# Block attention and cosine router on one core: paired first gathers, earlier key and embedding transposes, and logits in four column parts

## The chip, the cores and the metric

The kernel runs on one core of a Trainium2 chip. A core has a matrix engine (TensorE, "PE" in the profile, with its weight loads as "PEld"), VectorE (DVE), ScalarE (ACT), GpSimd (POOL) and SyncE (SP), which here does little but issue DMAs. Each engine runs its own instructions in order; semaphores tie them together. The metric is the device time of one execution in microseconds, the median of several runs. A profile is one execution more, with every instruction recorded.

## The reference, cut to what matters

```python
q, k, v: (4, 8, 768, 64)            # batch, heads, sequence, head size
mask: own block of 32 and its neighbours, first and last block rows and columns,
      and 3 sampled blocks per row of blocks
attn = softmax(where(mask, q @ k.T / 8, -1e9)) @ v
x = attn as (3072, 512)             # 8 heads side by side

xn = x / (norm(x) + 1e-6);  en = expert_emb / (norm(expert_emb) + 1e-6)
logits = xn @ en.T / tau            # (3072, 8)
expert_idx = argmax(logits);  gate = softmax(logits)[expert_idx]
out = gate * (relu(x @ w1[expert_idx]) @ w2[expert_idx])   # 8 experts, 512 -> 1024 -> 512
```

## The kernel before, in words

There are two large stages. The attention stage makes x and the routing; the expert stage gathers 128 rows of one expert at a time and sends them through that expert's two matrices. Everything is float32; one matrix product of that type is two pairs of a weight load and a matmul in the trace.

**Chunks, pairs and steps.** The 3072 rows are 24 chunks of 128 rows. Two chunks at the same place of two neighbouring sequences form a pair (`DUO = 2`), and a pair shares its block numbers. The order of chunks is `TURNS = [0, 2, 1, 3, 4, ...]`: the first chunks of the first two pairs come before their second chunks. `attention_fast` runs a loop of 25 steps `s`, in an order written out by hand: no scheduler moves anything, each engine gets its instructions in the order of the code. In step `s` four chunks are in work: `now` (scored in this step), `last` (its probabilities weigh the values), `past` (its rows x are transposed and its logits made) and `after` (its queries are transposed and its keys gathered, for the next step).

**Scores.** `score_near` makes the scores of the own and neighbouring blocks and of the two end blocks (tile `ac`, then `exp` into `pac`). `score_far` makes those of the sampled blocks (`dps`, then `pd`) from gathered keys `kg`, which `gather_k` copies together on GpSimd and VectorE out of the transposed keys `kt`. `turn_k(g)` transposes the keys of head pair `g` of a sequence (groups 0 to 3 are sequence 0, 4 to 7 sequence 1) into a bank of the two-bank ring `big`, which the scores use too; VectorE copies the even groups out, ScalarE the odd ones. `turn_q` transposes a chunk's queries.

**Weighing.** `weigh_far`, `weigh_near` and, for chunks at a sequence's end, `weigh_ends` multiply values by probabilities into `av` (all at L629). The far values come from HBM: `gather_v` issues one DMA for each sampled slot and block into a ring of two tiles, `vg`, one tile for each pair. Called with a third argument, it fetches for one chunk of the pair only (64 KB a DMA), without it for both (128 KB). The rows are runs of 256 bytes. All of these DMAs, and those for q, k, v, x and the weights, are issued by SyncE in the order of the code (`fetch_all`, L475 to L479), and a gather into `vg` waits until the products that read the tile two pairs before are done. A gather also needs its block number in a register first.

**Start of the stage.** Before the loop SyncE issues: keys of groups 0 to 3, values of two blocks, keys 4 and 5, the gathers of pair 0's first chunk, more values, keys 6 and 7, the gathers of pair 1's first chunk with the queries of the two second chunks between them, then the values of the second sequence, broken by the gathers of pair 0's second chunk, and at the end those of pair 1's second chunk. Keys 4 to 7 are transposed at the end of step 1, one after another, and only then are the keys for the next step gathered.

**Logits.** `normalize` divides by the sum of the probabilities into x and squares it on ScalarE into a tile `sq` for the norm. One step later `turn_x` transposes x into `xt`, and `chunk_logits` multiplies: the 128x128 parts of `xt` are the stationary operand, 8 columns of normalised embeddings `en` move, four products summed in one PSUM bank; ScalarE copies the (128, 8) result to `lg`. All small products of this stage share that one bank (`bank`, a ring of one tile). `build_experts` makes `en` in parts, called once before the loop, once in step 0 and twice in step 1. Its last two parts each transpose two pieces of the embeddings in that bank and copy them out.

**Routing** (`route`, `rank`, `dispatch_early`) is cut into pieces that hang on later steps; `planned(0)` runs such pieces in the middle of a step, `planned(1)` at its end.

Of the kernel before, what the change touches and what calls it, by code (L numbers as in the profile page):

```python
# [97 lines left out]
def build_consts(k):  # L98
    nc, pool = k.nc, k.const
    k.ones = pool.tile([P, P], F32, name="ones")  # L100
    nc.vector.memset(k.ones, 1.0)

    groups = k.ident.rearrange("p (g t) -> p g t", g=NG)
    k.mine = pool.tile([P, NG], F32, name="mine")
    nc.vector.reduce_sum(out=k.mine, in_=groups, axis=AX.X)
    no = iota(k, "group_no", [P, NG], [[1, NG]])
    k.group = pool.tile([P, 1], F32, name="group")
    nc.vector.tensor_tensor(out=no, in0=no, in1=k.mine, op=ALU.mult)
    nc.vector.reduce_sum(out=k.group, in_=no, axis=AX.X)
    k.ones_b = pool.tile([P, P], BF16, name="ones_b")  # L110
    nc.vector.memset(k.ones_b, 1.0)
    k.before = pool.tile([P, P], BF16, name="before")
    nc.gpsimd.memset(k.before, 1.0)
    nc.gpsimd.affine_select(out=k.before, in_=k.before, pattern=[[1, P]], compare_op=ALU.is_ge,
                            fill=0.0, base=-1, channel_multiplier=-1)
    k.rev = iota(k, "rev", [P, E], [[-1, E]], base=E)
    k.lane = iota(k, "lane", [P, P], [[1, P]])
    k.by_g = iota(k, "by_g", [P, NL + 1], [[G, NL + 1]])
    k.tile_no = iota(k, "tile_no", [P, NL], [[1, NL]])
    build_tokens(k, True)  # L120

    k.oh = pool.tile([P, NT, E], BF16, name="oh")
    k.rank = pool.tile([P, NT], F32, name="rank")
    k.seen = pool.tile([P, NT + 1, E], BF16, name="seen")
    nc.vector.memset(k.seen[:, 0, :], 0.0)
# [89 lines left out]
def build_experts(k):  # L215

    nc, pool = k.nc, k.setup
    emb, tau = k.emb_rows, k.tau_rows
    sq = pool.tile([E, DM], F32, name="emb_sq")
    nrm = pool.tile([E, 1], F32, name="emb_nrm")  # L220
    nc.scalar.activation(sq, emb, ACT.Square, accum_out=nrm)
    nc.gpsimd.tensor_tensor(out=nrm, in0=nrm, in1=k.half[0:E, 0:1], op=ALU.pow)
    yield
    nc.vector.tensor_scalar(out=nrm, in0=nrm, scalar1=1e-6, scalar2=tau[:, 0:1], op0=ALU.add, op1=ALU.mult)
    nc.vector.reciprocal(out=nrm, in_=nrm)
    nc.vector.tensor_scalar(out=emb, in0=emb, scalar1=nrm[:, 0:1], scalar2=None, op0=ALU.mult)
    yield
    k.en = k.const.tile([P, ND, E], F32, name="en")
    for some in (range(2), range(2, ND)):
        tp = bank(k, "tp")  # L230
        for c in some:
            nc.tensor.transpose(tp[:, c * E:(c + 1) * E], emb[:, c * P:(c + 1) * P], k.ident[0:E, 0:E])
        cols = slice(some.start * E, some.stop * E)
        nc.vector.tensor_copy(out=k.en.rearrange("p c e -> p (c e)")[:, cols], in_=tp[:, cols])
        yield


def load_pair(k, g, parts=(0, 1, 2)):
# [399 lines left out]
def weigh_near(k, n, turn):  # L638

    _, c, i = place(n)  # L640
    if turn == 0:
        k.av[n] = two_banks(k, "av"), set()
    e, st = k.pac[n], k.st_ring[n // DUO % 2]
    for hh in range(2 * turn, 2 * turn + 2):
        for h in (hh, hh + NPAIR):
            for half in (1,) if c == 0 else (0, 1):
                to = side(c, h, half)
                weigh(k, n, slice(D * to, D * (to + 1)), h, e[:, h // 2, half, D * (h % 2):D * (h % 2 + 1)],
                      st[:, half, i, h], turn == 1)
    if turn == 1:  # L650
        k.pac.pop(n)


def weigh_far(k, n, part):
# [14 lines left out]
def normalize(k, n):  # L669

    nc = k.nc
    b, c, i = place(n)
    s = n // DUO
    if i == 0:
        k.x[s] = k.xp.tile([P, DUO, ND, XE], F32, name="x", tag="x")
        k.nsq[s] = k.xp.tile([P, DUO], F32, name="nsq", tag="nsq")
        k.lg[s] = k.xp.tile([P, DUO, E], F32, name="lg", tag="lg")
    av = k.av.pop(n)[0].rearrange("p g (h w) -> p (g h) w", w=P)
    den = k.dens[:, n, :]
    nc.vector.tensor_scalar(out=den, in0=av[:, :, D], scalar1=1e-9, scalar2=None, op0=ALU.add)  # L680
    inv = k.xt_pool.tile([P, H], F32, name="inv", tag="inv")
    nc.vector.reciprocal(out=inv, in_=den)
    x = k.x[s][:, i, :, 0:P].rearrange("p j (h d) -> p j h d", h=2)
    half = NPAIR // 2
    if c:
        todo = [(slice(0, P), slice(0, P), slice(0, NPAIR))]
    else:
        todo = [(slice(0, P), slice(0, P), slice(0, half)), (slice(0, D), slice(D, P), slice(half, NPAIR)),
                (slice(D, P), slice(0, D), slice(half, NPAIR))]
    for to, at, pairs in todo:  # L690
        heads = slice(2 * pairs.start, 2 * pairs.stop)
        count = pairs.stop - pairs.start
        nc.vector.tensor_tensor(  # L693
            out=x[to, pairs], in0=av[at, heads, 0:D].rearrange("p (j h) d -> p j h d", h=2),
            in1=inv[at, heads].rearrange("p (j h) -> p j h", h=2).unsqueeze(3).broadcast_to(
                [at.stop - at.start, count, 2, D]), op=ALU.mult)
    sq = k.xt_pool.tile([P, ND, P], F32, name="sq", tag="sq", bufs=1)
    nc.scalar.activation(sq, k.x[s][:, i, :, 0:P], ACT.Square, accum_out=k.nsq[s][:, i:i + 1])


def turn_x(k, n):
# [6 lines left out]
    k.nc.vector.tensor_copy(out=t, in_=ps)  # L708


def chunk_logits(k, n):

    s, i = divmod(n, DUO)
    xt = k.xt.pop(n)
    ps = bank(k, "last_lg")
    for j in range(ND):
        k.nc.tensor.matmul(ps[:, 0:E], lhsT=xt[:, j], rhs=k.en[:, j, :], start=(j == 0), stop=(j == ND - 1))  # L717
    k.nc.scalar.copy(out=k.lg[s][:, i], in_=ps[:, 0:E])


# [25 lines left out]
def logits(k, x):  # L746
    nc, p = k.nc, k.rp
    lg = two_banks(k, "lg")[:, 0, 0:NC * E].rearrange("p (c e) -> p c e", e=E)
    for c2 in range(0, NC, 2):
        ps = k.big.tile([P, 2 * ND, P], F32, name="xt_ps", tag="big")  # L750
        for i in range(2 * ND):
            c, d = c2 + i // ND, i % ND
            nc.tensor.transpose(ps[:, i, :], x[:, c, d, 0:P], k.ident)
        xt = p.tile([P, 2 * ND, P], F32, name="xt")
        nc.vector.tensor_copy(out=xt, in_=ps)
        for c in (c2, c2 + 1):
            for d in range(ND):
                nc.tensor.matmul(lg[:, c, :], lhsT=xt[:, (c - c2) * ND + d, :], rhs=k.en[:, d, :],
                                 start=(d == 0), stop=(d == ND - 1))
    return lg  # L760

# [482 lines left out]
def attention_fast(n, ctx):  # L1244
# [40 lines left out]
    for vg in n.vg_ring:  # L1285
        nc.gpsimd.memset(vg[:, :, :, :, D:D + 1], 1.0)
    build_choice(n)
    fetch_all(n, gather_v(n, 0, 0), [])
    for m in range(2, NC):
        fetch_all(n, (), load_v(n, 0, m, 0))  # L1290
    turn_q(n, 0)
    for g in range(NPAIR):
        turn_k(n, g)
        if g + 6 < 2 * NPAIR:
            fetch_all(n, (), load_k(n, g + 6))
    fetch_all(n, gather_v(n, 1, 0), load_q(n, 0, 1) + load_q(n, 1, 1))
    for m in range(2):
        fetch_all(n, (), load_v(n, 0, m, 1))
    fetch_all(n, gather_v(n, 0, 1), [])
    for m in range(2, NC):  # L1300
        fetch_all(n, (), load_v(n, 0, m, 1))
    fetch_all(n, gather_v(n, 1, 1), [])
    build_bias(n)
    gather_k(n, 0)
    n.half = n.const.tile([P, NC], F32, name="half")
# [7 lines left out]
    nc.gpsimd.memset(zero, 0.0)  # L1313
    nc.sync.dma_start(n.x_dram[N:N + 1, :], zero)

    turning = {10: (8, 9), 11: (10, 11, 12), 12: (13, 14, 15)}
    keys_at = {2: (8, 9), 3: (10,), 4: (11,), 5: (12,), 6: (13,), 10: (14, 15)}
    values_at = {7: (0,), 8: (1,), 9: (2,), 11: (3,), 13: (4,), 15: (5,)}
    routed = {TURNS.index(DUO * b + 1) + 2: b for b in range(NS - 1)}
# [1 line left out]
    for s in range(NCH + 1):  # L1321
# [11 lines left out]
                gather_k(n, after)  # L1333

        ends = last is not None and place(last)[1] == 0
        late_keys = s == 1 or s in turning
        if now is not None:
            score_near(n, now)
            score_far(n, now)
# [26 lines left out]
            score_ends(n, last, 2)  # L1366
        if past is not None:
            turn_x(n, past)
        for g in turning.get(s, ()):
            turn_k(n, g)  # L1370
        if s in turning:
            keys_gathered()
        for part in range(2):
            if last is not None:
                weigh_far(n, last, part)
            if after is not None and part == 0 and not ends:
                turn_q(n, after)
        if ends:
            weigh_ends(n, last, (0, 2))
# [2 lines left out]
            if after is not None:  # L1382
                turn_q(n, after)
        if past is not None:
            chunk_logits(n, past)
        ahead, odd = s // DUO + 1, s % DUO
        loads, gathers = [], ()
        if s in (2, 3):
# [22 lines left out]
            weigh_ends(n, last, (1, 3))  # L1411
        if last is not None:
            weigh_near(n, last, 1)
            normalize(n, last)
        if s == 0:
            build_consts(n)
            next(experts)
        if s == 1:
            for g in range(NPAIR, 2 * NPAIR):
                turn_k(n, g)  # L1420
            keys_gathered()
            next(experts)
            next(experts)
            setup.close()
            n.dp = pool("dp_e", 1)
# [77 lines left out]
def fast(n):  # L1503
    n.rings, n.loads = {}, 0
    with ExitStack() as ctx:
# [24 lines left out]
            yield  # L1530

        def last_route():
            chunk_logits(n, NCH - 1)
            with n.tc.issue_after(n.relu):
                for _ in route(n, NS - 1):
                    pass
# [117 lines left out]
```

## Time and profile before

| | us |
|---|---|
| median of 3 runs | 645.87 (643.56 to 647.22) |
| the profiled execution | 645.84 |
| its span, first to last instruction | 644.0 |
| TensorE busy in the span | 607.3 (94%) |
| VectorE, ScalarE, GpSimd busy | 235.6, 141.6, 244.5 |
| last weighing product of the attention (L629) | about 277 |
| expert products in one unbroken row, from about | 294 |
| logits of one chunk on TensorE (L717, 8 instructions) | 0.99 |

The profile counts microseconds from the first instruction. "x32" is the number of instructions in a group. A bracket gives the idle time of the engine just before, and what ended it. In a table by windows the columns are: window, its length, busy time and number of instructions of PE, PEld, DVE, ACT and POOL, the mean granted TensorE clock (1.00 is full speed), the mean busy share of the core's 16 DMA engines (it can exceed 1 where the packets' times overlap), and GB/s moved. A list of waits gives the engine that waited, on what, for how many us in total, how many times, and the longest. SPq rows are DMA issues on SyncE: their length is the time that SyncE spent on issuing, not that of the transfer.

### The profile page before, as it was taken

Reading aid. Unit: us, or ns where it says so; the run is one execution under the profiler, and the core shown is the slowest. Engines: PE = TensorE matmul, PEld = TensorE weight load, DVE = VectorE, ACT = ScalarE, POOL = GpSimd, SP = SyncE. Lnnn points to the kernel's source line nnn. Section 1 sums busy time; section 2 is a strip of 40 time slices with the busy share of each in tenths; the row PEclk is TensorE's granted clock in tenths of the full one; section 3 lists DMA queues with packets and bytes.
Section 4 is the critical chain, followed back from the end, with each engine's and each line's share of the span. In section 5 each row is a group of like instructions: output and inputs, shape, how many; then the busy total and the mean of one; then the engine's idle time right before and its main releaser. Section 6 shows DMA issues by size and latency. Waiting matters only on the chain.

```text
span 644.0 us, 18357 instructions
## 1 busy us (share of the span) xinstructions
PE 607.3 (94%) x7496; PEld 471.4 (73%) x7496; DVE 235.6 (37%) x740; ACT 141.6 (22%) x286; POOL 244.5 (38%) x472
## 2 busy tenths in 40 slices
PE   6879889899999999999999999999999999999995
PEld 3668878798899888887777777663677746667773
DVE  3545544656666675236622111221121121211110
ACT  1534444554554444210000000000000000000000
POOL 1618246534766532031033444333334433333332
PEclk7899979999999799999999999999999999999998
DMA  9877999999999994079999999999899998999611
GB/s 170 170 150 152 177 170 170 183 185 175 182 191 184 178 162 145 36 278 401 396 406 394 406 399 365 341 320 375 308 395 410 396 375 308 413 390 408 247 48 34
DMA packets 187599, 170.57 MB, mean 265 GB/s; under 512 B 148008, under 2 KB 148136, under 8 KB 184690
## 3 DMA queue, kind: packets, MB, share of 16 engines
q1 hardware_dynamic: 180194, 155.35, 84.8%
q0 software_dynamic: 5216, 13.43, 5.7%
q8 instruction: 61, 1.00, 0.7%
q10 hardware_dynamic: 2096, 0.52, 0.5%
q14 instruction: 32, 0.26, 0.2%
HBM read 156.65 MB, written 12.90 MB: 263 GB/s over the span
## 4 chain that ended last, share of the span: by engine, by line
PE 75%; DMA 7%; SPq 6%; DVE 5%; issue 2%; POOL 2%; ACT 1%; POOLq 0%; DVEq 0%; ACTq 0%
PE hp L1152 25%; PE yp L1165 23%; PE av L629 6%; SPq L477 5%; PE dps L574 4%; PE yp L717 3%; DMA vg<-in_v_dram 3%; PE hp L1197 2%; PE yp L1217 2%; PE ac L549 2%; PE xg_ps L513 2%; PE ac L552 2%; DMA w<-in_moe_w_dram 2%; DMA qraw<-in_q_dram 1%; DMA kraw<-in_k_dram 1%
## 5 line engine op out<-in xcount | busy, mean ns | idle before, releaser
L1152 PEld LDWEIGHTS hp<-xgt,w 128*128 128x128 f32 x1472 | 167.8, 192 | 11.5 <-issue 10.2
L1152 PE MATMUL hp<-xgt,w 128*128 128x128 f32 x1472 | 169.2, 275 | 1.0 <-DMA w<-in_moe_w_dram 1.0
L1165 PE MATMUL yp<-w,h 128*128 128x512 f32 x368 | 161.9, 592 | 0.0
L1165 PEld LDWEIGHTS yp<-w,h 128*128 128x128 f32 x368 | 68.1, 190 | 76.5 <-issue 72.0
L1076 POOL DMA_INDIRECT xg<-x_dram,quarter x88 | 89.4, 1016 | 32.3 <-issue 27.4
L1178 POOL DMA_INDIRECT out_dram<-y,slot_l x20 | 20.5, 1026 | 155.8 <-DVE y L1177 155.8
L1155 ACT ACTIVATE h<-hp 128x512 f32<-128x512 f32 x23 | 13.7, 597 | 284.1 <-PE hp L1152 226.6
L1159 DVE TENSOR_SCALAR h<-hp 128x512 f32<-128x512 f32 x23 | 15.9, 692 | 145.1 <-PE hp L1152 145.1
L489 POOL COPY vg<-vt 32x1040 f32<-32x1040 f32 (+1 forms) x45 | 43.1, 958 | 57.2 <-PE av L629 45.0
L531 POOL COPY kg<-kt 128x128 f32 x176 | 43.2, 291 | 45.5 <-ACT kt L502 38.0
L549 PE MATMUL ac<-qt,kt 128*64 128x128 f32 x352 | 47.0, 290 | 3.3 <-DVE qt L518 3.3
L574 PEld LDWEIGHTS dps<-qt,kg 128*64 128x64 f32 x1408 | 48.2, 142 | 0.8 <-POOL vg L489 0.8
L574 PE MATMUL dps<-qt,kg 128*64 128x64 f32 x1408 | 46.9, 226 | 0.5 <-DVE kg L531 0.5
L552 PE MATMUL ac<-qt,kt 128*64 128x256 f32 (+1 forms) x192 | 46.4, 389 | 0.8 <-ACT kt L505 0.8
L518 DVE COPY qt<-xg_ps 64x512 f32<-64x512 f32 x48 | 33.0, 688 | 36.3 <-PE xg_ps L513 36.0
L1177 DVE TENSOR_SCALAR y<-yp,gate 128x512 f32<-128x512 f32 x20 | 15.0, 751 | 85.0 <-PE yp L1165 72.9
L549 PEld LDWEIGHTS ac<-qt,kt 128*64 128x64 f32 x352 | 41.5, 147 | 4.2 <-ACT st L441 1.8
L579 ACT ACTIVATE pd<-dps,bias 128x256 f32<-128x256 f32 x88 | 34.7, 475 | 15.8 <-PE dps L574 15.8
L629 PE MATMUL av<-vg,pd 128*32 128x65 f32 x1408 | 32.4, 225 | 3.5 <-DMA vg<-in_v_dram 2.8
L629 PE MATMUL av<-st,pac 128*64 128x65 f32 x704 | 31.0, 229 | 2.3 <-DVE x L693 1.3
L629 PEld LDWEIGHTS av<-vg,pd 128*32 128x32 f32 x1408 | 23.8, 110 | 12.1 <-issue 8.8
L708 DVE COPY xt<-xg_ps 128x512 f32<-128x512 f32 x24 | 16.6, 690 | 31.8 <-PE xg_ps L706 31.7
(229 smaller groups left out, 633.7 us busy)
## 6 DMA issues: line engine op xcount, KB each, us to landing
w<-in_moe_w_dram SPq DMA_DIRECT2D x52, 2048.0 KB
vg<-in_v_dram SPq DMA_DIRECT2D x114, 128.0 KB
kraw<-in_k_dram SPq DMA_DIRECT2D x32, 192.0 KB
x_dram<-x SPq DMA_DIRECT2D x10, 516.0 KB
qraw<-in_q_dram SPq DMA_DIRECT2D x9, 512.0 KB
w<-in_moe_w_dram SPq DMA_DIRECT2D x8, 512.0 KB
vt<-in_v_dram SPq DMA_DIRECT2D x10, 256.0 KB
vt<-in_v_dram SPq DMA_DIRECT2D x5, 512.0 KB
```

The lines of the kernel that those rows point to most:

```text
L477: k.nc.sync.dma_start(out=to, in_=src)
L489: k.nc.gpsimd.tensor_copy(out=k.vg_ring[s % 2][NRAND * BLK:P, g, which(i)], in_=k.vt[m][rows, which(i)])
L518: k.nc.vector.tensor_copy(out=t[rows, :, h], in_=ps[rows])
L531: copy(out=t[:, :, g, s * BLK:(s + 1) * BLK], in_=kt[:, :, bass.ds(shift, BLK)])
L549: nc.tensor.matmul(out[0:D, j, half], lhsT=kt[:, j, at:at + D], rhs=qt[:, j, :, D * half:D * (half + 1)], start=True, stop=True)
L552: nc.tensor.matmul(out[D:P, j, half:2].rearrange("p f h t -> p h f t"), lhsT=kt[:, j, S:S + D], rhs=qt[:, j, :, D * half:P].rearrange("p h ...
L574: nc.tensor.matmul(out[D * r:D * (r + 1), NG * j + g], lhsT=kg[:, j, g, D * r:D * (r + 1)], rhs=qt[:, j, :, cols], start=True, stop=True)
L579: nc.scalar.activation(e[:, :, g].rearrange("p j h t -> p j (h t)"), out.rearrange("p (j g) h t -> p j g (h t)", g=NG)[:, :, g], ACT.Exp, ...
L629: k.nc.tensor.matmul(av[lanes, h // NPAIR, h % NPAIR * P:h % NPAIR * P + D + 1], lhsT=lhsT, rhs=rhs, start=first[0], stop=last, skip_group ...
L1076: k.nc.gpsimd.indirect_dma_start(out=x[:, g], out_offset=None, in_=quarters, in_offset=bass.IndirectOffsetOnAxis(ap=k.quarter[:, g, t:t + ...
L1152: nc.tensor.matmul(hp[:, f, :], lhsT=w1[:, d, (f0 + f) * P:(f0 + f + 1) * P], rhs=xt[:, d, :], start=(d == 0), stop=(d == ND - 1))
L1165: nc.tensor.matmul(yp, lhsT=h[:, f, :], rhs=w2[:, f, :], start=(f == 0), stop=(f == NF - 1))
```

## The change

It has four parts.

1. *Gathers.* The first two pairs' values are gathered for both chunks at once. The 6 + 12 + 6 + 12 gathers of 64 KB become 6 + 12 of 128 KB, at the places where the first chunks' gathers stood. The values of the second sequence follow in one row.
2. *Keys.* Groups 4 and 5 are turned in step 0, after that step's queries, and groups 6 and 7 in step 1 in front of the far products. The keys for step 2 are gathered right after that.
3. *Embeddings.* All four pieces are transposed in one bank and copied once; `en` is padded with zeros from 8 to 32 columns, and `build_experts` has one part fewer, so that step 1 calls it once and not twice. The zero fill is on GpSimd.
4. *Logits.* `part_logits` takes the embeddings (32 columns, 24 of them zero) as the stationary operand and lets `xt` move: four products of 128 columns, each into its own 32 rows of the bank, one for each quarter of the 512 columns of x. ScalarE copies the (128, 128) result to `part`. After the second half of the near products `sum_logits` multiplies it by `sel`, a constant matrix that picks and sums the four quarters, and ScalarE copies (128, 8) to `lg`. The last chunk, which is routed in the expert stage, keeps the old form (`last_logits`). The square in `normalize` goes into the used `pac` tile and not into a tile of its own, so `pac` is given back there.

```diff
 def build_consts(k):
+    k.sel = pool.tile([P, E], F32, name="sel")
+    nc.vector.reduce_sum(out=k.sel, in_=groups[:, :, 0:E].rearrange("p g e -> p e g"), axis=AX.X)
...
 def build_experts(k):
+    k.en = k.const.tile([P, ND, BLK], F32, name="en")
+    nc.gpsimd.memset(k.en, 0.0)
...
-    k.en = k.const.tile([P, ND, E], F32, name="en")
-    for some in (range(2), range(2, ND)):
-        tp = bank(k, "tp")
-        for c in some:
-            nc.tensor.transpose(tp[:, c * E:(c + 1) * E], emb[:, c * P:(c + 1) * P], k.ident[0:E, 0:E])
-        cols = slice(some.start * E, some.stop * E)
-        nc.vector.tensor_copy(out=k.en.rearrange("p c e -> p (c e)")[:, cols], in_=tp[:, cols])
-        yield
+    tp = bank(k, "tp")
+    for c in range(ND):
+        nc.tensor.transpose(tp[:, c * E:(c + 1) * E], emb[:, c * P:(c + 1) * P], k.ident[0:E, 0:E])
+    nc.vector.tensor_copy(out=k.en[:, :, 0:E], in_=tp[:, 0:ND * E].rearrange("p (c e) -> p c e", e=E))
+    yield
...
 def normalize(k, n):
-    sq = k.xt_pool.tile([P, ND, P], F32, name="sq", tag="sq", bufs=1)
-    nc.scalar.activation(sq, k.x[s][:, i, :, 0:P], ACT.Square, accum_out=k.nsq[s][:, i:i + 1])
+    used = k.pac.pop(n)[:, 0:NPAIR:2].rearrange("p j f w -> p j (f w)")
+    nc.scalar.activation(used.rearrange("p j (e w) -> p j e w", w=P),
+                         k.x[s][:, i, :, 0:P].rearrange("p (j e) w -> p j e w", e=2), ACT.Square,
+                         accum_out=k.nsq[s][:, i:i + 1])
...
+def part_logits(k, n):
+    xt = k.xt.pop(n)
+    ps = bank(k, "part_lg")
+    for j in range(ND):
+        k.nc.tensor.matmul(ps[BLK * j:BLK * (j + 1), 0:P], lhsT=k.en[:, j], rhs=xt[:, j], start=True, stop=True)
+    k.part = k.xt_pool.tile([P, P], F32, name="part", tag="part", bufs=1)
+    k.nc.scalar.copy(out=k.part, in_=ps[:, 0:P])
+
+def sum_logits(k, n):
+    s, i = divmod(n, DUO)
+    ps = bank(k, "sum_lg")
+    k.nc.tensor.matmul(ps[:, 0:E], lhsT=k.part, rhs=k.sel, start=True, stop=True)
     k.nc.scalar.copy(out=k.lg[s][:, i], in_=ps[:, 0:E])
...
 def attention_fast(n, ctx):
-    fetch_all(n, gather_v(n, 0, 0), [])
+    fetch_all(n, gather_v(n, 0), [])
...
-    fetch_all(n, gather_v(n, 1, 0), load_q(n, 0, 1) + load_q(n, 1, 1))
-    for m in range(2):
+    fetch_all(n, gather_v(n, 1), load_q(n, 0, 1) + load_q(n, 1, 1))
+    for m in range(NC):
         fetch_all(n, (), load_v(n, 0, m, 1))
-    fetch_all(n, gather_v(n, 0, 1), [])
-    for m in range(2, NC):
-        fetch_all(n, (), load_v(n, 0, m, 1))
-    fetch_all(n, gather_v(n, 1, 1), [])
...
-    turning = {10: (8, 9), 11: (10, 11, 12), 12: (13, 14, 15)}
+    turning = {0: (4, 5), 1: (6, 7), 10: (8, 9), 11: (10, 11, 12), 12: (13, 14, 15)}
...
-        late_keys = s == 1 or s in turning
+        late_keys = s in turning and s > 0
...
+        if s == 0:
+            turn_q(n, after)
         for g in turning.get(s, ()):
             turn_k(n, g)
-        if s in turning:
+        if late_keys:
             keys_gathered()
         for part in range(2):
             if last is not None:
                 weigh_far(n, last, part)
-            if after is not None and part == 0 and not ends:
+            if after is not None and s and part == 0 and not ends:
                 turn_q(n, after)
...
         if past is not None:
-            chunk_logits(n, past)
+            part_logits(n, past)
...
         if last is not None:
             weigh_near(n, last, 1)
+        if past is not None:
+            sum_logits(n, past)
+        if last is not None:
             normalize(n, last)
...
         if s == 1:
-            for g in range(NPAIR, 2 * NPAIR):
-                turn_k(n, g)
-            keys_gathered()
-            next(experts)
             next(experts)
```

More of the change, by code (lines that the diff above doesn't have):

```diff
@@ L649, in weigh_near @@
                       st[:, half, i, h], turn == 1)
-    if turn == 1:
-        k.pac.pop(n)
 def weigh_far(k, n, part):
@@ L708, in turn_x, with last_logits @@
     k.nc.vector.tensor_copy(out=t, in_=ps)
-def chunk_logits(k, n):
+def last_logits(k, n):
     s, i = divmod(n, DUO)
@@ L716, in chunk_logits @@
     for j in range(ND):
-        k.nc.tensor.matmul(ps[:, 0:E], lhsT=xt[:, j], rhs=k.en[:, j, :], start=(j == 0), stop=(j == ND - 1))
+        k.nc.tensor.matmul(ps[:, 0:E], lhsT=xt[:, j], rhs=k.en[:, j, 0:E], start=(j == 0), stop=(j == ND - 1))
+    k.nc.scalar.copy(out=k.lg[s][:, i], in_=ps[:, 0:E])
+def part_logits(k, n):
[9 more added lines that the diff above has]
+    k.nc.tensor.matmul(ps[:, 0:E], lhsT=k.part, rhs=k.sel, start=True, stop=True)
     k.nc.scalar.copy(out=k.lg[s][:, i], in_=ps[:, 0:E])
@@ L757, in logits @@
             for d in range(ND):
-                nc.tensor.matmul(lg[:, c, :], lhsT=xt[:, (c - c2) * ND + d, :], rhs=k.en[:, d, :],
+                nc.tensor.matmul(lg[:, c, :], lhsT=xt[:, (c - c2) * ND + d, :], rhs=k.en[:, d, 0:E],
                                  start=(d == 0), stop=(d == ND - 1))
@@ L1532, in last_route @@
         def last_route():
-            chunk_logits(n, NCH - 1)
+            last_logits(n, NCH - 1)
             with n.tc.issue_after(n.relu):
```

## The prediction

> **What bounds the kernel now.** I first read the span and the table of slices, then the chain of waits. From 294 us on the chain is one run of expert products (hp and yp at L1152 and L1165, 48% of the span) with TensorE 100% busy. The change touches nothing there, so what it is worth is decided before 283 us, and the rest slides. Next I read SyncE's issues in order of time over the first 70 us:
>
> ```profile
> 36.46 5.92 SPq L477 DMA_DIRECT2D vg<-in_v_dram  x8
> ...
> 44.15 4.41 SPq L477 DMA_DIRECT2D vg<-in_v_dram  x6
> ...
> 51.87 9.04 SPq L477 DMA_DIRECT2D vg<-in_v_dram  x12
> ...
> 61.39 0.41 SPq L479 DMA_DIRECT2D qraw<-in_q_dram  x1
> 61.84 5.12 SPq L479 DMA_DIRECT2D kraw<-in_k_dram  x4
> ```
>
> A 64 KB gather takes about 0.74 us of SyncE's queue (5.92/8, 4.41/6, 9.04/12), that is 87 GB/s, so while gathers are issued the DMA engines run dry. Stage by stage (us, then busy time of PE, PEld, DVE, ACT, POOL; clock; DMA share; GB/s):
>
> ```profile
> 20.00:25.00 5.00, 2.97 (x40) 2.66 (x41) 3.50 (x17) 3.17 (x7) 4.04 (x13) 0.76 0.45 101
> 40.00:45.00 5.00, 3.31 (x30) 2.78 (x26) 3.56 (x7) 1.90 (x4) 0.00 (x0) 1.00 0.53 120
> 55.00:60.00 5.00, 5.00 (x140) 4.55 (x136) 3.14 (x8) 4.17 (x10) 4.75 (x11) 1.00 0.45 99
> 65.00:70.00 5.00, 3.09 (x78) 2.96 (x70) 1.38 (x2) 1.18 (x3) 0.00 (x0) 1.00 0.93 204
> ```
>
> After 65 us this is over: in windows of 5 us and more the share stays at 0.83 to 1.40, at about 177 GB/s on the mean of 60 to 220 us. SyncE's own waits between 60 and 225 us sum to only some 11 us in 165, in pieces like
>
> ```profile
> SPq L477 <- PE dps L574: 2.1, 4, 0.8
> SPq L477 <- PE av L629: 1.6, 3, 1.1
> ```
>
> so the stream of loads runs back to back there, TensorE (busy 93%) is in step with it, and the chain passes through it three times in stretches of 15 us (110 to 125, 148 to 168, 184 to 202 us), each ending in a wait for vg. The last gather that the stream itself delays is issued at about 223 us; from there to 283 us TensorE leads. Three regimes: SyncE's issue up to 61 us, DMA rate up to 223, TensorE after it.
>
> Last, TensorE's stops, in its order of time:
>
> ```profile
> 67.06 0.63 PE L513 MATMUL xg_ps<-ident,qraw 128*128 128x128 f32 x4 [1.91 <-DMA qraw<-in_q_dram]
> 83.76 0.27 PE L629 MATMUL av<-vg,pd 128*32 128x65 f32 x2 [0.54 <-DMA vg<-in_v_dram]
> ```
>
> and in the table by windows what follows the second of them:
>
> ```profile
> 84.00:86.00 2.00, 0.58 (x5) 0.28 (x4) 0.00 (x0) 1.77 (x2) 1.92 (x7) 1.00 1.23 184
> 86.00:88.00 2.00, 1.78 (x54) 1.52 (x58) 0.52 (x1) 0.00 (x0) 0.85 (x4) 0.81 1.38 168
> 88.00:90.00 2.00, 2.00 (x28) 1.83 (x18) 0.86 (x2) 0.00 (x0) 0.00 (x0) 0.50 1.44 167
> ```
>
> The reader sees late loads stop TensorE, and after the second stop the granted clock is 0.50 until 94 us.
>
> **Gathers paired.** 36 gathers of 64 KB become 18 of 128 KB: 18 x 0.74 = 13.3 us less of SyncE's queue before 61 us, the bytes unchanged. The bytes set the floor: from 19 to 61 us about 6.3 MB are asked for; at 178 GB/s they take 35.4 us and would be in at 54.5 instead of 61.4, 7 us earlier; at 200 GB/s (reached in 10 to 20 us) 10. So q for the third pair, issued at 61.39, comes 7 to 10 us sooner and the 1.91 us stop at 67.06 goes. The next thing SyncE issues, the gathers for the third pair (68.18 us), waits for the fourth step's far products (done by 60.8 us before) to free the ring. They go out at about 60: the stream is 8 us ahead. I take 8, with ends 3 and 10.
>
> **Keys turned in steps 0 and 1.** Twelve L500 instructions per two groups take 1.53 us on TensorE. Groups 4 and 5 fall into step 0's gap (23.2 to 24.76, a 1.57 us wait for qt), but VectorE copies group 4 (0.96 us) after both qt copies (to 24.64), so the next product into that bank starts 0.9 us late. Groups 6 and 7 go in front of step 1's far products, and everything behind them on TensorE waits if their data is late. Their loads are issued from 26.55 to 31.4, landing some 3.6 us later (as qraw did, 33.94 to 37.6), so to 35; the six gathers ahead now carry 0.39 MB more, 2 us, so about 36.5 to 37. TensorE is ready at about 33: a stop of 3 to 4 us takes the place of the 1.5 us at 36.1, the 0.9 and 1.4 between the key copies at 40 to 43, and the roughly 2 us that step 2 waited for copied keys at 44.7 to 46.6. The gather of keys behind it on GpSimd (12 copies, 2.95 us) then lies under step 1's products. Net on TensorE: 2 us gained, ends -2 and +4. The loss needs the clock. The Trainium skill (TensorE: Matmul & The Clock Gate, part 1 on the HAM clock gate) drops the clock to half after an idle window of about 3.4 us; by it the stop at 83.4 to 86.2 us, broken up by small products, is too short. The row disagrees: some 2.4 us idle cost 6.8 us at 0.50, so 3.4 us more. By the rule my early stop costs only itself; by the row 3.4 us on top. I count that as a risk: before, 2 us of idle between 36 and 38 us left the clock at 1.00.
>
> **Embeddings.** Transposes in one bank: the 1.7 us wait of the second pair for VectorE's copy is gone (inside the 2 us above). The zero fill of en is about 0.2 us of GpSimd (as ident's, 128x128), in its 0.90 us idle before L222; uncovered it costs that. sel is one reduction of about 0.2 us on an idle VectorE.
>
> **Logits.** Now 8 instructions in 0.99 us per chunk (137.05 to 138.04), 124 ns each, set by loading xt as 128x128 weights. The far products, also 32 columns wide in four column parts, run 16 with 65 moving columns in 0.59 us, 37 ns each; at 128 columns 73, so four parts take 0.29 us, with filling 0.33. If nothing overlapped, 8 x 115 ns (the hp products' pace) = 0.92. The sum is two instructions of the old kind, 0.25. One more change of column width per step: the Trainium skill (TensorEngine Tiling (Array Packing), key properties) says that a change of tiling mode drains the array, which speaks against this. A 65-column product lasts 0.22 us at 0.04 spacing, so a drain is at most 0.18: 23 x 0.18 = 4.1 us by the rule. The steps hold such changes now and no gap stands beside them, so I take 0.1. Together 0.68: 0.31 saved per chunk, with ends +0.45 and -0.5.
> The new wait: sum_logits stands in TensorE's order behind half of the near products (0.5 us) and waits for ScalarE's copy of part. That copy lies between lg (128x8, 0.166 us) and kt (128x768, 0.80): about 0.27. Last part's drain 0.25 + 0.27 + handovers = 0.6, against 0.5 of cover: 0.1 exposed. Behind sum_logits are the next chunk's scores. ScalarE is free at that point:
>
> ```profile
> ACT lg L718 <- PE yp L717: 42.0, 21, 4.5
> ```
>
> 2 us idle before lg in 21 of 23 chunks. A rank or dispatch product that takes the bank right after the sum now waits about 0.4 us for lg's copy, in some four steps. So 0.2 to 0.3 per chunk remain, and seven chunks lie after 223 us (steps 18 to 24): 2 us. The other 16 save 4 us where the loads lead, which gives nothing. Square into the old pac tile: same engine, same size, its bank's next writer is ScalarE itself: nothing.
>
> **Sum.** Against the profiled execution (645.84 us, span 644.0; the median of three is 645.87, the same): the stream 8 earlier up to 223 us, the tail 2: 635.8, taken as 635.5. The stops at 67 and 84 us and the half clock after the latter go too, about 8 us of TensorE, but they only let it follow the stream; what is late next is vg again, in steps 9, 13 and 17.
>
> **Rivals.**
> 1. Forecast, 46%: as above, 631.5 to 640.
> 2. TensorE leads all along, 24%: the stream is not at its floor in 65 to 223 us but in step with TensorE. Then its gains add: start 2, q 1.9, the stop at 84 us 2.2 and its half clock 3.4, other waits for vg 1, 23 x 0.3 = 7: 17.5, 628. For it: 93% busy and rates up to 192 GB/s. Against it: SyncE waits so little.
> 3. The start gives nothing, 19%: keys 6 and 7 land late, the clock halves, TensorE reaches the third pair as late as before and frees the ring no sooner. The tail and part of the stops remain: 3 to 4, 642.
> 4. Slower, 7%: the sum's wait. If the copy of part queues behind the pair of st copies (2.12 us at 143.83), TensorE stands about 1.2 us per chunk in 23 chunks: 23 x (1.2 - 0.3) = 21 lost, 8 + 2 gained: about 656. It decides from 0.75 us per chunk (0.3 + 10/23). Against it: ScalarE's idle time above.
> The remaining 4%: a further half-clock spell, either side of no change.
>
> A measurement here tells about 0.5% (3.2 us) from no change. Faster by more: 1 and 2 whole and most of 3: 0.84; within: 0.09; slower: 0.07. The range for 8 in 10, from 2's end to 3's: 627.5 to 642.5.
>
> **What would show it.** DMA share near 1 from 25 us; no gather under 128 KB; q for the third pair issued by 54 us; the gathers for the third pair by 61; no stop at 84 us; the logits' products under 0.7 us per chunk; TensorE waits for vg at steps 9 to 17, more than 2.8 us in all. If those waits are gone, rival 2 holds; if TensorE stands before L736 for more than 0.3 us, 4; if keys 6 and 7 stop it past 38 us, 3. The prediction is wrong if the attention's end (283 us) moves by other than 6 to 14 us.

## The result, and the profile after

| | before | after |
|---|---|---|
| median, us | 645.20 (4 runs) | 638.64 (4 runs, 636.4 to 640.67) |
| ratio of the times, 95% interval | | 0.9896 [0.9851, 0.9941] |
| profiled execution, us | 645.84 | 636.40 |
| span of the profile, us | 644.0 | 634.7 |
| weights of the first full row of expert products asked for, us | 283.50 | 274.07 |
| TensorE busy | 607.3 | 597.9 |

The kernel is faster by 1.0%, 6.6 us. The changed kernel was measured twice more beside the experiments: 636.7 (0.9861 [0.9792, 0.993]) and 637.45 (0.9879 [0.9832, 0.9926]); over the three the gain is 6.6 to 9.1 us. The expert stage slides along: the profiled span shrinks by 9.3 us and the attention's end, marked by the request for those weights, moves by 9.4.

First SyncE's issues in order of time, the rows that answer to those of before (start, us, engine, line, what):

```profile
38.04 6.88 SPq L478 DMA_DIRECT2D vg<-in_v_dram  x8
44.97 8.23 SPq L480 DMA_DIRECT2D vt<-in_v_dram  x7
...
53.83 1.07 SPq L480 DMA_DIRECT2D qraw<-in_q_dram  x1
54.95 5.38 SPq L480 DMA_DIRECT2D kraw<-in_k_dram  x4
...
61.53 3.50 SPq L478 DMA_DIRECT2D vg<-in_v_dram  x2
```

Eight paired gathers take 0.86 us each and carry twice the bytes, 152 GB/s where the single ones made 87. The query of the third pair goes out at 53.8 (61.4 before), the third pair's gathers at 61.5 (68.2 before): 6.7 us sooner. The table by windows of the changed kernel shows the DMA engines now near full (columns as before; the last row is from a finer cut). On the mean of 19 to 54 us they move 175 GB/s at a share of 1.02, which points to the bytes and no longer to the issue:

```profile
20.00:25.00 5.00, 4.58 (x43) 4.43 (x44) 4.81 (x15) 3.17 (x7) 4.48 (x14) 0.50 0.88 166
...
40.00:45.00 5.00, 4.92 (x120) 4.25 (x118) 0.79 (x2) 1.62 (x2) 2.16 (x10) 0.98 0.89 155
...
55.00:60.00 5.00, 5.00 (x143) 4.47 (x141) 0.87 (x3) 4.20 (x8) 4.64 (x8) 1.00 1.07 216
...
65.00:70.00 5.00, 5.00 (x100) 4.54 (x102) 3.40 (x10) 1.63 (x5) 1.57 (x2) 1.00 1.14 175
...
86.00:88.00 2.00, 2.00 (x76) 2.00 (x74) 1.58 (x11) 1.11 (x2) 1.01 (x6) 1.00 1.37 182
```

The holes of 0.45 and 0.53 in the DMA share are filled, TensorE no longer stops between 65 and 70 us, and between 84 and 94 us it is busy at a clock of 1.00. In its order of time there are new stops, though:

```profile
33.83 0.85 PE L501 MATMUL kps<-ident,kraw 128*128 128x128 f32 x6 [1.01 <-DMA kraw<-in_k_dram]
...
36.80 1.51 PE L501 MATMUL kps<-ident,kraw 128*128 128x128 f32 x6 [2.12 <-DMA kraw<-in_k_dram]
...
98.06 0.30 PE L630 MATMUL av<-vg,pd 128*32 128x65 f32 x2 [0.57 <-DMA vg<-in_v_dram]
...
99.42 0.61 PE L630 MATMUL av<-vg,pd 128*32 128x65 f32 x26 [1.05 <-DMA vg<-in_v_dram]
```

The first two are keys 6 and 7, turned before they have landed; the second two are a later step's gathers. Between 60 and 225 us the list of waits has TensorE standing for vg about as long as before (2.8 us), in spite of the stream's lead:

```profile
PE av L630 <- DMA vg<-in_v_dram: 3.0, 6, 1.1
PE av L630 <- DVE x L825: 2.3, 1, 2.3
```

The second row is a load again in disguise. VectorE's x could not be written until the store of an older x from the same ring had gone out (VectorE's row at 107.93 us waited 5.43 us for it), and that store stands in SyncE's order behind the gathers. Before, this wait cost TensorE 0.9 us. In the two further profiles of the changed kernel the two rows read 3.3 and 2.6, and 3.2 and 2.3 us.

One thing in the profile of the kernel before was overlooked by the prediction. After two idle times of TensorE of 0.44 and 0.91 us (210.4 to 212.3 us) the clock was 0.50 once more:

```profile
212.00:214.00 2.00, 1.75 (x39) 1.53 (x40) 1.37 (x2) 0.00 (x0) 0.70 (x1) 0.89 1.33 181
214.00:216.00 2.00, 2.00 (x24) 1.98 (x26) 0.26 (x3) 0.17 (x1) 1.88 (x5) 0.50 1.18 283
218.00:220.00 2.00, 2.00 (x31) 2.00 (x29) 1.93 (x12) 0.86 (x1) 1.65 (x6) 0.50 1.28 148
```

The step in it took 12.2 us, from the far scores at 206.68 to the next at 218.87; the same step of the changed kernel takes 8.0 (201.98 to 209.97). So 4.2 of the 9.3 us between the two profiles arise in this one step. No other profile here has such a stretch between 170 and 250 us, so it is not part of every execution.

### The profile page after: what moved, and what is told of

Read it like the earlier page. It is cut to its first block, busy times and chain, and to the rows that moved or that the text cites. A ratio compares the mean times of both kernels' runs of the same rounds, so it can differ in the third digit from the quotient of the medians.

```text
span 634.7 us, 18413 instructions
## 1 busy us (share of the span) xinstructions
PE 597.9 (94%) x7542; PEld 456.8 (72%) x7542; DVE 235.6 (37%) x740; ACT 148.9 (23%) x309; POOL 244.8 (39%) x473
## 4 chain that ended last, share of the span: by engine, by line
PE 75%; DMA 8%; SPq 7%; DVE 4%; ACT 3%; issue 2%; POOL 1%; POOLq 0%; DVEq 0%; ACTq 0%
PE hp L1171 25%; PE yp L1184 24%; PE av L630 7%; SPq L478 5%; DMA vg<-in_v_dram 4%; PE dps L575 3%; PE hp L1216 2%; PE yp L1236 2%; DMA kraw<-in_k_dram 2%; PE ac L550 2%; PE xg_ps L514 2%; DMA w<-in_moe_w_dram 2%; PE ac L553 1%; PE bps L597 1%; PE kps L501 1%
## 5 line engine op out<-in xcount | busy, mean ns | idle before, releaser
L550 PE MATMUL ac<-qt,kt 128*64 128x128 f32 x352 | 45.0, 280 | 2.3 <-DVE qt L519 2.0
L553 PE MATMUL ac<-qt,kt 128*64 128x256 f32 (+1 forms) x192 | 44.4, 375 | 0.8 <-ACT kt L506 0.8
L550 PEld LDWEIGHTS ac<-qt,kt 128*64 128x64 f32 x352 | 38.5, 139 | 3.8 <-issue 2.2
L630 PEld LDWEIGHTS av<-st,pac 128*64 128x64 f32 x704 | 25.3, 137 | 8.2 <-issue 8.1
```

What stands on the lines that cost most here:

```text
L550: nc.tensor.matmul(out[0:D, j, half], lhsT=kt[:, j, at:at + D], rhs=qt[:, j, :, D * half:D * (half + 1)], start=True, stop=True)
L553: nc.tensor.matmul(out[D:P, j, half:2].rearrange("p f h t -> p h f t"), lhsT=kt[:, j, S:S + D], rhs=qt[:, j, :, D * half:P].rearrange("p h ...
L630: k.nc.tensor.matmul(av[lanes, h // NPAIR, h % NPAIR * P:h % NPAIR * P + D + 1], lhsT=lhsT, rhs=rhs, start=first[0], stop=last, skip_group ...
```

## The experiments

The theory: from about 65 to 223 us the stream of loads leads, and TensorE's gains in that time turn into waits. The rival: TensorE leads, and the gains of the parts add. The ratios are against the kernel before, run beside each.

A profile here is one execution, and the start of the stage differs from one to the next: the kernel before with half of its gathers left out, up to there the same program, reached the far scores of step 4 at 74.70 us, the kernel before at 71.83. The verdicts therefore rest on the times; the profiles show where a wait stands.

**The logits alone.** Gathers, keys and embeddings stay in their old places.

```diff
 (kernel before)
-            chunk_logits(n, past)
+            part_logits(n, past)
...
+        if past is not None:
+            sum_logits(n, past)
```

> The kernel before with the new logits alone (column parts, sum product, square into the used pac tile; gathers, keys and embedding transposes in their old places). Stream theory (the loads lead from 65 to 223 us): only the chunks after 223 us count, about 7 x 0.35 us, so 2 to 3 us less than before, and TensorE's waits for vg grow beyond the 2.8 us of before. Rival (TensorE leads all along): 23 x 0.35 us, so 7 to 8 us less.

Measured 643.39, 0.9961 [0.9942, 0.998]: 2.5 us less, as the theory had it; the rival's 7 to 8 are excluded. Its list of waits, 60 to 225 us, shows the rest:

```profile
PE av L632 <- DMA vg<-in_v_dram: 4.2, 4, 2.1
PE av L632 <- DVE x L827: 3.6, 1, 3.6
```

Both have grown, from 2.8 and 0.9.

**The gathers alone.**

```diff
 (kernel before)
-    fetch_all(n, gather_v(n, 0, 0), [])
+    fetch_all(n, gather_v(n, 0), [])
...
-    fetch_all(n, gather_v(n, 1, 0), load_q(n, 0, 1) + load_q(n, 1, 1))
+    fetch_all(n, gather_v(n, 1), load_q(n, 0, 1) + load_q(n, 1, 1))
...
```

> The kernel before with the paired gathers alone. Stream theory: the gathers for the third pair are issued near 61.5 us (68.2 before), the stop for q at 67 us and the stop and half clock at 84 to 94 us are gone, and the whole is 5 to 7 us below before: most of what the whole change brings. Rival (gains of the parts add, the gathers bring only the stop for q): 2 us.

Measured 639.06, 0.992 [0.9893, 0.9948]: 5.2 us less by the ratio, most of the whole. The third pair's gathers go out at 61.36. Its profile has no wait of TensorE for vg at all between 60 and 225 us, and SyncE stands for other engines for 17 us there, 11 before; the two longest rows:

```profile
SPq L477 <- PE av L629: 5.5, 3, 2.8
SPq L477 <- PE xg_ps L706: 2.3, 1, 2.3
```

So the lead is not fixed. In this profile the stream comes out just ahead and TensorE leads; the two are that close. TensorE's own delay helps: the gathers now carry twice the bytes ahead of a query that step 1 needs, and it stood for that query, longer than the 1.54 us of before:

```profile
39.70 1.09 PE L513 MATMUL xg_ps<-ident,qraw 128*128 128x128 f32 x4 [3.39 <-DMA qraw<-in_q_dram]
```

The clock was 0.50 from there to 43.1 us.

**Keys and embeddings alone.**

```diff
 (kernel before)
-    turning = {10: (8, 9), 11: (10, 11, 12), 12: (13, 14, 15)}
+    turning = {0: (4, 5), 1: (6, 7), 10: (8, 9), 11: (10, 11, 12), 12: (13, 14, 15)}
...
```

> The kernel before with keys and embeddings turned in the other steps alone. Stream theory: SyncE still reaches the third pair's q at about 61 us and its gathers at 68, so within 1 us of before, whatever TensorE gains by then. Rival: step 1 ends about 2 us sooner and the whole is 2 us less.

Measured 645.51, 1.0001 [0.9981, 1.0021]: nothing, and the rival's 2 us are excluded. The list of waits shows where TensorE stood:

```profile
PE xg_ps L511 <- DMA qraw<-in_q_dram: 4.3, 1, 4.3
```

The stop for the third pair's query was 1.9 us before. TensorE arrives 0.9 us sooner (its last products ahead of the query start at 63.28, before at 64.22), and in this execution SyncE issued the query 2.4 us later (63.74, before 61.39). After the stop the clock was 0.50 from 69.1 to 76.0 us.

**The whole change with the old logits.**

```diff
 (changed kernel)
-            part_logits(n, past)
+            last_logits(n, past)
...
-        if past is not None:
-            sum_logits(n, past)
```

> The changed kernel with the old logits (128x128 stationary, 8 columns moving), gathers and keys as changed. Stream theory: 2 to 3 us slower than the changed kernel, so about 641, with fewer TensorE waits for vg before 220 us. Rival: 7 to 8 us slower than the changed kernel, about 646, no gain left.

Measured 638.00, 0.9887 [0.9846, 0.9927]. Against the changed kernel's 0.9896, 0.9861 and 0.9879 no difference can be told: the 7 to 8 us of the rival are excluded, the 2 to 3 us of the theory are neither shown nor excluded. TensorE's waits for vg are 1.6 us here against 3.0 with the new logits (3.3 and 3.2 in its other two profiles).

**Less to load.** Every other gather of sampled values is left out from step 4 on, in the kernel before, in the changed kernel, and in the changed kernel with the old logits.

```diff
             gathers = coming if odd else islice(coming, 6)
+            if ahead > 2:
+                gathers = list(gathers)[::2]
```

> The kernel before with every other gather of sampled values left out from the fourth pair of chunks on (steps 4 and later), so that the loads have slack; nothing else is changed, stale values are weighed. Stream theory: TensorE runs at its own pace from about step 6 on, its stops for vg and the half clock after them (before 223 us) go, 5 to 9 us less than before. Rival (TensorE leads): less than 2 us.

> The changed kernel with the same gathers left out. Stream theory: with the loads out of the way every chunk's shorter logits count, so it lies 9 to 13 us below the kernel before with the same gathers left out, a larger distance than the 6.6 us between the full kernels. Rival: the distance is the same 6 to 7 us.

> The changed kernel with the old logits and with every other gather of sampled values left out from the fourth pair on (steps 4 and later). Stream theory: where the loads have slack the shorter logits count in every chunk, 23 x 0.4 us, so it is 7 to 10 us slower than the changed kernel with the same gathers left out (626.35), about 634 to 636, although with all gathers the old and the new logits differed by less than can be told. Rival (the new logits gain nothing anywhere, the waits they add eat it): within 2 us of 626.35.

| | with all gathers, ratio | with half of them |
|---|---|---|
| kernel before | 1 | 0.991 [0.9881, 0.9939], 640.51 us |
| changed, old logits | 0.9887 [0.9846, 0.9927] | 0.9857 [0.9807, 0.9907], 635.77 us |
| changed kernel | 0.9896 [0.9851, 0.9941] | 0.9704 [0.9636, 0.9773], 626.35 us |

The kernel before gains 5.3 us (645.78 to 640.51; 5 to 9 expected). With slack in the loads the changed kernel falls by another 10 us and lies 14 us under the kernel before, more than the 9 to 13 expected; the new logits, worth nothing that can be told with all gathers, are worth 9 us (635.77 - 626.35, not measured side by side, so give or take some 5). SyncE's waits between 60 and 225 us sum to 61 us in the changed kernel with half of the gathers, 12 with all of them. This decides between theory and rival: with all gathers the loads take away what the logits save. It does not tell bytes from issues, since both were left out together; the full DMA share after 65 us speaks for the bytes.

The pair of runs also separates TensorE's saving from the rest. The logits rows of two successive steps, with the old logits and half the gathers:

```profile
164.63 1.06 PE L718 MATMUL yp<-en,xt 128*128 128x8 f32 x8
...
172.93 1.06 PE L718 MATMUL yp<-en,xt 128*128 128x8 f32 x8
```

and with the new ones:

```profile
165.74 0.40 PE L727 MATMUL yp<-xt,en 128*32 128x128 f32 x8
...
166.69 0.39 PE L736 MATMUL yp<-sel,part 128*128 128x8 f32 x2
...
173.73 0.40 PE L727 MATMUL yp<-xt,en 128*32 128x128 f32 x8
```

A step lasts 8.30 us with the old and 7.99 with the new: 0.31 per chunk, 7 us over 23 chunks. Whether the other 2 of the 9 us are more than noise is not shown; the profile with the old logits has the clock at 0.50 from 144.3 to 147.7 us, the one with the new logits has none after 40. In the three profiles with half of the gathers TensorE has no row for vg in its list of waits between 60 and 225 us; waits without a named cause come to 0.8 to 2.8 us.

**Keys 6 and 7 loaded ahead of the first gathers.**

```diff
 (changed kernel)
-    fetch_all(n, gather_v(n, 0), [])
-    for m in range(2, NC):
-        fetch_all(n, (), load_v(n, 0, m, 0))
     turn_q(n, 0)
     for g in range(NPAIR):
         turn_k(n, g)
...
+    fetch_all(n, gather_v(n, 0), [])
+    for m in range(2, NC):
+        fetch_all(n, (), load_v(n, 0, m, 0))
```

> The changed kernel with the loads of key groups 6 and 7 issued ahead of the first pair's gathers and the values behind them. The stop of 3.1 us for keys in step 1 and the half clock after it go, so step 1 ends 4 to 6 us sooner on TensorE. Stream theory: SyncE reaches the third pair's gathers no sooner, so the whole stays within 1.5 us of the changed kernel. Rival: 4 to 6 us less than the changed kernel.

> The changed kernel with the loads of key groups 6 and 7 ahead of the first gathers, once more for a narrower interval. Stream theory: within 1.5 us of the changed kernel beside it. Rival: 4 to 6 us less.

Measured 635.41 beside the changed kernel's 636.7, and 636.47 beside its 637.45: 1.0 to 1.3 us under it each time, within what these runs can't tell from nothing (0.9864 [0.9816, 0.9913] against 0.9879 [0.9832, 0.9926]). The stop for keys has gone, and another stands one step later. In the second of the two profiles, in TensorE's order of time:

```profile
46.43 0.27 PE L630 MATMUL av<-vg,pd 128*32 128x65 f32 x2 [1.87 <-DMA vg<-in_v_dram]
...
47.30 0.27 PE L630 MATMUL av<-vg,pd 128*32 128x65 f32 x2 [0.60 <-DMA vg<-in_v_dram]
```

four such stops together 4.3 us, and after them the clock is at 0.70 on the mean of 50 to 55 us. The third pair's gathers go out at 61.55, no sooner. In this order too TensorE stands for loads, only elsewhere: 4.3 us here, 3.1 us in the changed kernel's step 1. What fewer bytes would do at the start was not measured.

**The changed kernel again,** as the level for the others:

> The changed kernel once more, beside the others of this call: 636 to 641 as before, the level that the three others are held against.

> The changed kernel beside the two others of this call: 636 to 640.

636.70 and 637.45. A fourth buffer for x, which might take away the wait for the store, was not tried. No version was found that beats the changed kernel by more than the runs can tell.

## Why the prediction was right

The forecast was 635.5 us, 10 us less than before; measured were 638.6, 6.6 less, inside its own range of 631.5 to 640. The mechanism holds: the loads lead, the start of the stage frees them, and the logits count only where the loads have slack. The sizes come out less well, point by point.

- **SyncE's issue binds before 61 us, bytes after it.** Right. The DMA share fills up, q goes out at 53.8 ("by 54") and the third pair's gathers at 61.5 ("by 61").
- **The stream is 8 us ahead.** This is the term that was too large. Over its start it came out 6.7 us ahead (68.18 to 61.53), near the floor of 7 that the bytes gave at 178 GB/s. The prediction had put the issue at 60, taking only TensorE's release of the ring into account; SyncE reached the gathers no sooner, since the keys and queries ahead of them take 7 us of a queue that is full. The gathers alone are worth 5.2 us in the times. Nor did the lead last: the gathers that SyncE issued at 204.69 before go out at 200.55, 4.1 us sooner (3.6 and 0.6 in the two other profiles). Why it shrinks was not traced.
- **Keys: 2 us on TensorE, a stop of 3 to 4 us in step 1.** The stops are 1.01 and 2.12 us, the second until 36.8 ("36.5 to 37"). The 2 us gained are not there. The last products ahead of the third pair's query, before and after:

```profile
64.22 0.93 PE L605 MATMUL bps<-qt,kt 64*64 64x64 f32 x48
64.03 0.93 PE L606 MATMUL bps<-qt,kt 64*64 64x64 f32 x48
```

  That is 0.2 us sooner; in the two other profiles of the changed kernel they start at 65.09 and 65.23, later than before. The next far scores do start 2.0 us sooner (69.83, before 71.83), but that is the stop of 1.91 us for the query, and its end is the gathers' doing. With the gathers alone these products start at 67.76, so beside paired gathers the keys may be worth something to TensorE; whether the whole gains by it can't be told (0.992 for the gathers alone, 0.9887 with keys and embeddings). The sum of the forecast counted nothing for this term, so the miss did not show in it.
- **The clock after that stop.** Weighed as a risk, and it came: after 3.1 us of idle time, cut in two by a product, the windows of the changed kernel read

```profile
36.00:38.00 2.00, 1.20 (x6) 1.14 (x6) 0.00 (x0) 0.00 (x0) 0.00 (x0) 0.69 0.95 167
38.00:40.00 2.00, 2.00 (x48) 1.58 (x48) 0.82 (x4) 1.30 (x3) 0.79 (x4) 0.50 1.02 171
```

  As in the row at 84 us before (2.2 us idle in all, where the prediction says 2.4), no single gap reached the 3.4 us of the rule (the Trainium skill, TensorE: Matmul & The Clock Gate, part 1 on the HAM clock gate); the row was the better guide. From 36 to 42 us (clock 0.69, 0.50 and 0.95) it took about 1.7 us from TensorE, an estimate; in the two other profiles of the changed kernel the clock was 0.50 for 6.8 us, twice as long.
- **Logits: 0.31 us per chunk.** Right for the step with slack (8.30 to 7.99), and so was that they count only where TensorE leads: 2.5 us for the part alone, by the times. At the logits themselves 0.24 of it is seen: from their start to the next scores' start TensorE took 1.50 us before (137.05 to 138.55) and takes 1.26 now (131.25 to 132.51); the other 0.07 us lie elsewhere in the step and were not traced. The column parts take 0.33 us as estimated. From the near products' start to the sum it is 0.62 us, where these products took 0.51 before: 0.1 of the wait for part's copy (0.27 us, as estimated) is exposed. The sum with its change of column width takes 0.31, taken as 0.25 + 0.1: beyond the 0.25 of two instructions of the old kind, the drain that the Trainium skill names (TensorEngine Tiling (Array Packing), key properties) is at most about 0.06 us here, an estimate. The bank costs 0.8 us in three waits of rank products for lg, where four of 0.4 were expected.
- **What is late next is vg.** Right: 3.0 us in all, against "more than 2.8", in steps 7, 9, 11 and 13, where 9, 13 and 17 had been named. It was not foreseen that with the gathers alone these waits vanish altogether, that is that the lead of the stream is so thin; nor that the store of x becomes a wait of its own.
- **The tail, 2 us.** With the logits alone 2.5 us in the times, where six chunks and not seven lie after 223 us. The pair of profiles can't confirm it: there TensorE's lead over the kernel before grows from 4.7 us (206.68 to 201.98) to 9.4 at the end, 4.2 of it in the one step of the half clock before. That the profiles come out 9.4 us apart, so near to the forecast of 10, is in part luck: the stream brought less than 8, and a stretch that nobody had counted brought the rest.

Rival 2 (628 us) lies near what the changed kernel ran with half of the gathers, 626. Of rival 3 the first half happened: keys 6 and 7 landed late, the clock halved, and TensorE reached the third pair's query no sooner to speak of. Its conclusion failed, since SyncE, and not TensorE, had held the third pair's gathers: they went out 6.7 us sooner all the same. Rival 4 did not happen: the sum's wait is 0.1 us.

## What to carry to other kernels

When two resources run in step, each of them near full, look for the time in which the leading one is starved, and not for the largest saving on the other: 18 issues saved on a queue brought 5 us, 7 us of TensorE work saved brought 2.5. To learn which leads, take away half of the suspected load, even at the price of the result, and see whether the other edits begin to count. And an edit worth nothing today can be the next one's gain: with half of the gathers these logits brought 9 us.

## What the runs showed of the hardware

- The clock fell to 0.50 after one unbroken idle time of 3.39 us (gathers alone, to 39.7 us) or 4.29 us (keys alone, to 68.5 us), but also after less: 1.01 and 2.12 us with 0.85 us of products between (changed kernel, 33 to 37 us), four stops of 0.5 to 0.6 us with single products between (before, 83 to 86 us), 0.44 and 0.91 us (before, 210 to 212 us). One wait of 1.91 us (before, 65 to 67 us) left it at 1.00. These stretches at 0.50 lasted 3.4 or 6.8 us.
- A gather of 64 KB with a block number from a register took SyncE 0.74 us, one of 128 KB 0.86 us with the DMA engines at a share of about 0.9.
- Four products of 128 columns with 32 stationary columns, each in its own column part, took 0.33 us together, where one product of 128 columns over the full array takes 0.23 (two hp instructions at 115 ns).
